# Attention by column norms and a top-1 mixture of experts on one core: hand-outs one row group sooner, raw weights in pieces, norms in columns

## The chip, the cores and the metric

The kernel runs on one core of a Trainium2 chip. Its time is device microseconds (us) of one execution. Three runs of the kernel before took 1202.16, 1208.28 and 1210.1 us; the median is 1208.28. The profiled execution is a separate one.

## The reference

For each of 4 batches, q, k and v are 5056 x 256. Norms run over the 5056 rows (`axis=1`), so the attention matrix is 256 x 256:

```python
qn = q / (np.linalg.norm(q, axis=1, keepdims=True) + 1e-06)
kn = k / (np.linalg.norm(k, axis=1, keepdims=True) + 1e-06)
s = kn.transpose(0, 2, 1) @ qn / tau
a = np.exp(s - s.max(-1, keepdims=True))
a /= a.sum(-1, keepdims=True) + 1e-09
x = (v @ a).reshape(20224, 256)
e_idx = np.argmax(x @ w_gate, axis=1)          # 8 experts
# out[i] = prob(e) * sigmoid(x_i @ w_output_gate)[e] * (relu(x_i @ w1[e]) @ w2[e]), w1 256x1024, w2 1024x256
```

## The kernel before, in words

**Gram.** `gram(b)` loads q and k in 20 steps of two 128-row tiles (tag `qk`, 6 buffers), squares and adds them for the norms (L353, L354), and multiplies k by q in fp32 (L366): the Gram product. After the last step it sums the squares over the partitions (L381 for q as a row of 256, L383 for k as two columns), takes the root on ScalarE (L389), refines and inverts it in seven VectorE instructions on 258 columns (L390 to L397), scales, and makes the softmax, its transpose and the product with the gate matrices. Pauses (`HOLD`) stand between these, so that other work comes in between.

**Mixing.** `mix(b)` makes v @ a in 20 steps of 256 rows: four transposes of v (L477), twelve matmuls (L506 to L508), the copies L481, L483 and L509. A row group is four steps (1024 rows; the fifth and last group has 960). After each group `route` finds each row's expert, counts ranks within the expert with small matmuls (L576, L579), and eight indirect DMAs of GpSimd scatter the rows, 256 values and gates, to the expert's region in DRAM (L598).

**Hand-out.** `checkpoint(n)` reads the counts so far. It orders the experts by size (`rank_experts`), writes a mark behind the scatters (L615), and makes a table of the next blocks of 256 tokens (`table`, `weights`): checkpoint 0 after `mix(1)` gives 4 blocks, checkpoint 1 after `mix(2)` gives 10, checkpoint 2 the rest. Before the last one, only blocks that are full for certain may be given out; `FIRST[r]` is the first block that may use the expert of rank r: 0, 4, 11, 18, 25, 32, 39, 46.

**Weights.** `prep` loads an expert's two matrices (1 MB each, L273, L276), and `split` squares and sums them for a scale (L297), then makes a high and a low fp16 half (L310 on ScalarE, L311 on VectorE) and stores both to DRAM (L316). Rank 0 is split in place into the weight buffer; the others go by one buffer `sp` and one `sl`. The raw matrices of ranks 0 and 1 use the tag `raw` (3 buffers, shared with the hidden activations `hb` of a block); the later ones use `st`, the buffers of mixed rows.

**Blocks.** `blocks` runs one block in four turns of PE work: h = relu(x w1) in three fp16 products (L919 to L921), y = h w2 likewise (L942 to L944). Rows are fetched on SP's queue (L843, into `qk` buffers), transposed by DMA on SP's queue (L885), weights are fetched on GpSimd's queue where the expert changes (L825), results scattered (L954).

**Order.** The program's order is written by hand with Python generators: the loops at L1012 to L1055 step `mix`, and beside each step draw so many steps of the Gram work (`ahead`, `GRATE` 1.3), of `prep` and of `run` (the blocks). The framework's planner then orders each engine's instructions by its own cost estimates, within the dependences. Each engine, and each engine's queue of DMA issues, then works through its instructions in that order. Counting `yield`s: a `mix` has 23, a `gram` 32; before, Gram work lasts until about step 10 of `mix(2)`; `run` is drawn from step `OPEN` = 10 on, and its first nine draws (`FAR` 5, then 1 + `XP` + `NEAR`) hold no matmuls.

```python
    some = checkpoint(0)
    next(some)                                  # ranks, counts, mark: after mix(1)
    preps = prep(0, AHEAD)
    for b in range(SOON, B - 1):                # b = 2
        for i, _ in enumerate(_steps(mix(b), (ahead, GRATE), (preps, PRATE))):
            if i == LATE: finish(some); opened[0] += 1     # table
            if i >= OPEN: next(run)
```

Of the kernel before, what the change touches and what calls it, by code (L numbers as in the profile page):

```python
# [20 lines left out]
P = 128  # L21
BLK = 256
BIG = 4194304
EXP_MASK = 0x7F800000

# [19 lines left out]
def tile_colnorm_attention_then_top1_moe(  # L45
# [45 lines left out]
    sure = [-(-(n * N - E * (BLK - 1)) // BLK) for n in (SOON, B - 1)]  # L91
# [165 lines left out]
    def prep(first, end):  # L257
# [3 lines left out]
        def gather():  # L261
            r, half = jobs[len(raws)]
            if r > AHEAD:
                raw = wk.tile([P, R, CW], F32, tag="st", name=f"raw{r}_{half}", bufs=STB)
                raw = raw.rearrange("p r w -> p (r w)")[:, :HW1]
            else:
                raw = big.tile([P, HW1], F32, tag="raw", name=f"raw{r}_{half}", bufs=3)
            row = nc.values_load(
# [3 lines left out]
            if half == 0:  # L272
                nc.sync.dma_start(raw, wraw[0][bass.ds(row, P), :])  # L273
            else:
                rows = wraw[1][bass.ds(row, P), :].rearrange("(f a) (b d) -> (a b) f d", f=FC, d=C)
                nc.sync.dma_start(raw.rearrange("p (f d) -> p f d", f=FC), rows)  # L276
            raws.append(raw)

        for n, (r, half) in enumerate(jobs):
            while len(raws) < min(n + DEEP, len(jobs)):  # L280
                gather()
                yield
            yield from pause(LAG if n == 0 else REST)
            yield from split(raws[n], half, r)

    def split(raw, half, r):
# [8 lines left out]
        for i in range(2):  # L295
            a = slice(i * HW1 // 2, (i + 1) * HW1 // 2)
            nc.scalar.activation(hi[:, a], raw[:, a], AF.Square, accum_out=ss[:, i : i + 1])  # L297
# [9 lines left out]
        src, dh, dl = raw, hi, lo  # L307
        cuts = [(slice(None), slice(i * HW1 // 2, (i + 1) * HW1 // 2)) for i in range(2)]
        for i, a in enumerate(cuts):
            nc.scalar.activation(dh[a], src[a], AF.Copy, scale=sw)  # L310
            nc.vector.scalar_tensor_tensor(  # L311
                out=dl[a], in0=src[a], scalar=sw, in1=dh[a], op0=ALU.mult, op1=ALU.subtract
            )
# [11 lines left out]
    def gram(b):  # L325
# [55 lines left out]
        nc.tensor.matmul(k_ps[:, :C], onesf, both[:, 0, :], start=True, stop=True, skip_group_check=True)  # L381
        for c in range(CC):
            nc.tensor.matmul(  # L383
                k_ps[:, C + c : C + c + 1], both[:, 1, c * P : (c + 1) * P], onesf[:, 0:1],
                start=False, stop=c == CC - 1, skip_group_check=True,
            )
        ss = k_ps[:, : C + CC]
        root = one.tile([P, C + CC], F32, tag="root", name=f"root{b}")
        nc.scalar.activation(root, ss, AF.Sqrt)  # L389
        nc.vector.tensor_scalar(out=root, in0=root, scalar1=1e-30, scalar2=None, op0=ALU.max)  # L390
        r = one.tile([P, C + CC], F32, tag="rq", name=f"rn{b}")
        nc.vector.reciprocal(r, root)
        nc.vector.tensor_tensor(out=r, in0=ss, in1=r, op=ALU.mult)
        nc.vector.tensor_tensor(out=r, in0=r, in1=root, op=ALU.add)
        nc.vector.tensor_scalar(out=r, in0=r, scalar1=0.5, scalar2=1e-6, op0=ALU.mult, op1=ALU.add)
        nc.vector.tensor_scalar(out=r[:, C:], in0=r[:, C:], scalar1=tau_b, scalar2=None, op0=ALU.mult)
        nc.vector.reciprocal(r, r)  # L397
# [694 lines left out]
```

## Time and profile before

| what | value |
|---|---|
| median of three runs | 1208.28 us |
| profiled execution | 1209.88 us, of which the span 1208.1 us |
| TensorE (PE) busy | 1174.4 us (97%) |
| VectorE (DVE) / ScalarE (ACT) / GpSimd (POOL) busy | 748.5 / 602.3 / 517.9 us |
| mean granted TensorE clock | 0.990 of 2.4 GHz |
| DMA | 208.56 MB |

The span is from the first instruction to the last. A busy PE here is PE with matmuls under way; the table by stage below shows where it stood idle, and at which clock.

### The profile page before, as it was taken

The numbers are of one execution on the slowest core, as the hardware profiler recorded it, in microseconds if no ns is written. First come the engines' busy times: TensorE is split into PE (matmuls) and PEld (weight loads), VectorE is DVE, ScalarE is ACT, GpSimd is POOL, SyncE is SP. The second block draws the span as 40 slices with busy tenths as digits, with TensorE's granted clock in tenths as the row PEclk, the third lists the DMA queues.
The fourth block names the chain that finished last, engine by engine and source line by source line (L and its number), as shares of the span: only waits on it lengthen the run. The fifth ranks groups of instructions, "written<-read, shape, count | busy, mean of one in ns | idle before, by whom it ended". The sixth has DMA issues, their size and how long they took to land.

```text
span 1208.1 us, 28097 instructions
## 1 busy us (share of the span) xinstructions
PE 1174.4 (97%) x10412; PEld 1066.4 (88%) x10412; DVE 748.5 (62%) x2300; ACT 602.3 (50%) x1193; POOL 517.9 (43%) x518
## 2 busy tenths in 40 slices
PE   8999999997997999999999999999999999999997
PEld 7899999887996888888888888888889999999997
DVE  7787768788685966566666654555554555555531
ACT  6576656576574555555556443333333444344432
POOL 0003756536565753333444433344444444444433
PEclk9999999998998999999999999999999999999999
DMA  9976888877767898657554436643325534336533
GB/s 319 330 246 207 301 277 259 295 242 215 212 242 236 223 264 178 150 147 174 148 137 126 112 80 113 182 76 77 72 63 176 112 73 82 79 81 197 168 104 130
DMA packets 186307, 208.56 MB, mean 173 GB/s; under 512 B 121832, under 2 KB 134510, under 8 KB 182200
## 3 DMA queue, kind: packets, MB, share of 16 engines
q1 hardware_dynamic: 145368, 139.41, 42.0%
q0 software_dynamic: 40512, 67.05, 18.9%
q8 instruction: 84, 1.38, 0.5%
q14 instruction: 55, 0.45, 0.1%
q10 hardware_dynamic: 288, 0.26, 0.1%
HBM read 281.84 MB, written 61.41 MB: 284 GB/s over the span
## 4 chain that ended last, share of the span: by engine, by line
PE 87%; DMA 6%; DVE 2%; issue 2%; ACT 1%; SPq 1%; POOL 0%; POOLq 0%; DVEq 0%; ACTq 0%
PE h_ps L919 11%; PE h_ps L921 11%; PE h_ps L920 11%; PE y_ps L942 11%; PE y_ps L943 11%; PE y_ps L944 11%; PE s_ps L366 10%; PE x_ps L506 3%; PE x_ps L508 2%; PE x_ps L507 2%; PE vt_ps L477 2%; DMA wbuf<-wsc,wi 1%; DMA qk<-in_k_dram 1%; DMA raw<-in_moe_w_dram 1%; DMA qk<-in_q_dram 1%
## 5 line engine op out<-in xcount | busy, mean ns | idle before, releaser
L924 DVE SCALAR_TENSOR_TENSOR hb<-h_ps,hb 128x512 f16<-128x512 f32 (+1 forms) x360 | 228.5, 636 | 276.0 <-ACT hb L923 275.1
L923 ACT ACTIVATE hb<-h_ps 128x512 f16<-128x512 f32 (+1 forms) x360 | 197.9, 552 | 364.1 <-PE h_ps L921 362.5
L919 PE MATMUL h_ps<-xt,wbuf 128*128 128x256 f16 (+1 forms) x1440 | 366.5, 262 | 3.0 <-ACT st L509 3.0
L921 PE MATMUL h_ps<-xt,wbuf 128*128 128x256 f16 (+1 forms) x1440 | 366.6, 262 | 0.0
L920 PE MATMUL h_ps<-xt,wbuf 128*128 128x256 f16 (+1 forms) x1440 | 366.5, 262 | 0.0
L942 PE MATMUL y_ps<-wbuf,hb 128*128 128x256 f16 x1296 | 353.3, 273 | 5.0 <-ACT yo L948 2.4
L944 PE MATMUL y_ps<-wbuf,hb 128*128 128x256 f16 x1296 | 353.3, 273 | 0.0
L943 PE MATMUL y_ps<-wbuf,hb 128*128 128x256 f16 x1296 | 353.3, 273 | 0.0
L825 POOL DMA_INDIRECT wbuf<-wsc,wi x172 | 177.8, 1034 | 404.5 <-PE h_ps L921 365.2
L598 POOL DMA_INDIRECT xs_d<-st,r_si x160 | 168.1, 1051 | 199.2 <-DVE r_d L550 101.9
L954 POOL DMA_INDIRECT out_dram<-yo,b_id x162 | 165.4, 1021 | 69.2 <-issue 42.3
L366 PE MATMUL s_ps<-qk 128*128 128x256 f32 x640 | 152.4, 390 | 5.8 <-DMA qk<-in_q_dram 3.9
L920 PEld LDWEIGHTS <-wbuf 128*128 128x128 f16 x1440 | 141.0, 98 | 16.9 <-issue 3.2
L919 PEld LDWEIGHTS <-wbuf 128*128 128x128 f16 x1440 | 142.1, 99 | 14.1
L921 PEld LDWEIGHTS <-wbuf 128*128 128x128 f16 x1440 | 141.1, 98 | 13.3
L943 PEld LDWEIGHTS <-hb 128*128 128x128 f16 x1296 | 126.8, 98 | 19.3 <-issue 5.6
L366 PEld LDWEIGHTS s_ps<-qk 128*128 128x128 f32 x640 | 121.4, 196 | 21.2 <-DMA qk<-in_k_dram 3.9
L944 PEld LDWEIGHTS <-hb 128*128 128x128 f16 x1296 | 126.8, 98 | 14.9
L942 PEld LDWEIGHTS <-hb 128*128 128x128 f16 x1296 | 126.8, 98 | 14.3
L354 DVE TENSOR_TENSOR acc<-acc,sq 128x1024 f32<-128x1024 f32 x76 | 92.9, 1223 | 46.8 <-ACT sq L353 45.4
L880 ACT ACTIVATE xr<-xg,b_sx 128x256 f16<-128x256 f32 x162 | 74.6, 502 | 66.8 <-DVE b_sx L233 46.4
L353 ACT ACTIVATE sq<-qk 128x1024 f32<-128x1024 f32 x76 | 80.3, 1060 | 53.0 <-DMA qk<-in_k_dram 44.8
(191 smaller groups left out, 1448.8 us busy)
## 6 DMA issues: line engine op xcount, KB each, us to landing
xg<-xs_d SPq DMA_DIRECT2D x72, 272.0 KB
qk<-in_q_dram SPq DMA_DIRECT2D x75, 256.0 KB
qk<-in_k_dram SPq DMA_DIRECT2D x75, 256.0 KB
v<-in_v_dram SPq DMA_DIRECT2D x32, 512.0 KB
raw<-in_moe_w_dram SPq DMA_DIRECT2D x16, 1024.0 KB
wsc<-whi SPq DMA_DIRECT2D x14, 512.0 KB
wsc<-wlo SPq DMA_DIRECT2D x14, 512.0 KB
v<-in_v_dram SPq DMA_DIRECT2D x8, 480.0 KB
```

The costliest lines, as they stand in the source:

```text
L366: nc.tensor.matmul(s_ps[:, c, :], kt[:, 1, t, c * P : (c + 1) * P], qt[:, 0, t, :], start=st == 0 and t0 == 0 and t == 0 and c == 0 and n ...
L598: ins = nc.gpsimd.indirect_dma_start(out=xs_d[:, :], out_offset=bass.IndirectOffsetOnAxis(ap=si[:np_, t : t + 1], axis=0), in_=st[:np_, t, ...
L825: nc.gpsimd.indirect_dma_start(out=wbuf[half][:, at_of(u), :], out_offset=None, in_=wsc[half][:end, :], in_offset=bass.IndirectOffsetOnAxi ...
L919: nc.tensor.matmul(hp, w1s[:, 0, c, fs], xh, start=fi == 0 and c == 0, stop=False, **KWM)
L920: nc.tensor.matmul(hp, w1s[:, 0, c, fs], xl, start=False, stop=False, **KWM)
L921: nc.tensor.matmul(hp, w1s[:, 1, c, fs], xh, start=False, stop=fin, **KWM)
L923: nc.scalar.activation(hh, h_ps[:, :, :w], AF.Relu)
L924: nc.vector.scalar_tensor_tensor(out=hb[:, 1, 2 * fp : 2 * fp + 2, :w], in0=h_ps[:, :, :w], scalar=0.0, in1=hh, op0=ALU.max, op1=ALU.subtract,
L942: nc.tensor.matmul(y_ps[:, t, :], hb[:, 0, f, tsl], w2s[:, 0, f, :], start=st, stop=False, **KWM)
L943: nc.tensor.matmul(y_ps[:, t, :], hb[:, 0, f, tsl], w2s[:, 1, f, :], start=False, stop=False, **KWM)
L944: nc.tensor.matmul(y_ps[:, t, :], hb[:, 1, f, tsl], w2s[:, 0, f, :], start=False, stop=fin, **KWM)
L954: ins = nc.gpsimd.indirect_dma_start(out=out[:, :], out_offset=bass.IndirectOffsetOnAxis(ap=un["id"][:, t : t + 1], axis=0), in_=un["yo"][ ...
```

## The change

1. **Hand-outs.** Checkpoints 0 and 1 are split over hooks in `mix(1)` and `mix(2)`: ranks and counts are read in step 18, before the last row group is counted; the mark is written at the end of the same `mix`, ahead of the last group's scatters; the table follows in step `LATE` = 1 (was 5) of the next. The last group's 960 rows are left out of the sure blocks, so `FIRST` becomes 0, 4, 11, 17, 23, 30, 36, 42. `OPEN` goes from 10 to 3.
2. **Raw weights.** Each raw matrix is loaded as two pieces of 512 KB, each half stored as soon as it is split; ranks from 2 on use the `v` buffers (4 of 512 KB) instead of `st`. `prep` of rank 0 starts in step 18 of `mix(1)`, of rank 1 in step 18 of `mix(2)`; then comes a pause of 22 draws.
3. **Norms.** Four column sums of one column each; an integer estimate and two Newton steps for the reciprocal root, plus one correction of the root, on 4 columns on VectorE in place of the ScalarE root; a diagonal matrix and an fp32 matmul bring q's factors back to a row.
4. **Rates.** 1.4 Gram steps to a step of `mix(0)` and `mix(1)` (was 1.3); other rates as below; rows are fetched at every turn of a block, not once per block.

```diff
-    sure = [-(-(n * N - E * (BLK - 1)) // BLK) for n in (SOON, B - 1)]
+    sure = [-(-(n * N - (N - (NG - 1) * GROUP) - E * (BLK - 1)) // BLK) for n in (SOON, B - 1)]
-    GRATE = 1.3
+    GRATE, AHEAD_RATE = 1.3, 1.4
-    DEEP, LAG, REST = 2, 3, 2
-    LATE, OPEN, MARKED = 5, 10, 3
+    DEEP, LAG, REST, SLOW = 2, 4, 1, 4
+    LATE, OPEN, MARKED, HOOKED = 1, 3, 3, 18
+    REST_AT = 22
-    BRATE = 0.7
+    BRATE = 0.72
-    MRATE = 1.2
-    WRATE = 0.8
+    MRATE = 1.8
+    WRATE = 1.0
...
             if r > AHEAD:
-                raw = wk.tile([P, R, CW], F32, tag="st", name=f"raw{r}_{half}", bufs=STB)
+                parts = [
+                    ld.tile([P, 4, C], F32, tag="v", name=f"raw{r}_{half}_{i}", bufs=VB).rearrange("p t c -> p (t c)")
+                    for i in range(2)
+                ]
...
+            for i, part in enumerate(parts):
+                if half == 0:
+                    nc.sync.dma_start(part, rows[:, i * HW1 // 2 : (i + 1) * HW1 // 2])
...
+                yield
...
-            yield from pause(LAG if n == 0 else REST)
+            yield from pause(LAG if n == 0 else SLOW if r > AHEAD + 1 else REST)
...
+            for n, part in enumerate((hi, lo)):
+                nc.sync.dma_start(wsc[half][rows, n * HW1 + a.start : n * HW1 + a.stop], part[:, a])
             yield
-        for n, part in enumerate((hi, lo)):
-            nc.sync.dma_start(wsc[half][rows, n * HW1 : (n + 1) * HW1], part)
...
-        nc.tensor.matmul(k_ps[:, :C], onesf, both[:, 0, :], start=True, stop=True, skip_group_check=True)
+        for i in range(2):
+            for c in range(CC):
+                n = i * CC + c
+                nc.tensor.matmul(
+                    k_ps[:, n : n + 1], both[:, i, c * P : (c + 1) * P], onesf[:, 0:1],
...
+        nc.vector.tensor_scalar(
+            out=y.bitcast(I32), in0=half, scalar1=-1.0, scalar2=float(RSQRT), op0=ALU.mult, op1=ALU.add
+        )
+        for _ in range(2):
+            t = t4("n_t")
+            nc.vector.tensor_tensor(out=t, in0=hss, in1=y, op=ALU.mult)
+            nc.vector.tensor_tensor(out=t, in0=t, in1=y, op=ALU.mult)
+            nc.vector.scalar_tensor_tensor(out=y, in0=t, scalar=1.5, in1=y, op0=ALU.add, op1=ALU.mult)
...
-        nc.scalar.activation(root, ss, AF.Sqrt)
...
-        nc.vector.reciprocal(r, root)
...
+        nc.vector.reciprocal(r, r)
+        dq = one.tile([P, CC, P], F32, tag="root", name=f"dq{b}")
         for c in range(CC):
+            nc.vector.tensor_scalar(out=dq[:, c, :], in0=ident, scalar1=r[:, c : c + 1], scalar2=None, op0=ALU.mult)
+        yield from pause(HOLD + 1)
+        n_ps = ps_x.tile([P, 512], F32, tag="x", name=f"n_ps{b}")
+        nc.tensor.matmul(n_ps[:, :C], onesf, dq.rearrange("p c m -> p (c m)"), start=True, stop=True)
+        yield
+        rq, rk = n_ps[:, :C], r[:, CC:]
...
+                adv("x", fetch_x, got["prep"] + QKB)
...
     for b in range(SOON, B - 1):
-        for i, _ in enumerate(_steps(mix(b), (ahead, GRATE), (preps, PRATE))):
+        for i, _ in enumerate(_steps(mix(b, hand[1]), (ahead, GRATE))):
+            if i < HOOKED:
+                due += PRATE
+                while due >= 1.0:
+                    due -= 1.0
+                    next(preps, None)
+            else:
+                if i == HOOKED:
+                    finish(preps)
+                    preps = chain(prep(AHEAD, AHEAD + 1), pause(REST_AT), prep(AHEAD + 1, E))
+                next(preps)
             if i == LATE:
-                finish(some)
+                finish(hand[0])
                 opened[0] += 1
             if i >= OPEN:
-                next(run)
+                some += 1.0 if i < OPEN + FAR + XP + 1 + NEAR else BRATE
+                while some >= 1.0:
+                    some -= 1.0
+                    next(run)
```

## Rows read from the trace of the kernel before

**Rows 1.** The page's first part: busy us, share of the span and instructions of each engine.

```profile
PE 1174.4 (97%) x10412; PEld 1066.4 (88%) x10412; DVE 748.5 (62%) x2300; ACT 602.3 (50%) x1193; POOL 517.9 (43%) x518
```

**Rows 2.** Busy time by stage. Columns: stage in us from the span's start, its length, busy us (and instructions) of PE, its weight loads, DVE, ACT, POOL, then the granted share of TensorE's clock, the DMA engines' busy share, and GB/s.

```profile
0.00:75.00 75.00, 69.16 (x321) 60.53 (x322) 55.45 (x80) 48.69 (x55) 2.72 (x19) 0.98 0.93 316
75.00:220.00 145.00, 144.52 (x1035) 135.72 (x1034) 107.66 (x289) 95.12 (x203) 74.45 (x69) 1.00 0.80 256
220.00:250.00 30.00, 25.91 (x176) 23.86 (x175) 18.39 (x78) 17.85 (x36) 12.09 (x13) 0.94 0.84 292
...
272.00:300.00 28.00, 20.84 (x169) 19.53 (x168) 22.28 (x87) 17.28 (x41) 16.53 (x18) 0.88 0.80 220
...
360.00:385.00 25.00, 17.44 (x131) 15.35 (x131) 14.13 (x62) 12.04 (x27) 12.73 (x13) 0.86 0.86 268
385.00:430.00 45.00, 43.36 (x404) 38.85 (x403) 37.55 (x153) 22.46 (x42) 34.76 (x33) 1.00 0.81 210
430.00:1184.00 754.00, 753.75 (x7311) 680.41 (x7310) 423.87 (x1287) 331.00 (x660) 312.20 (x305) 1.00 0.51 126
1184.00:1208.10 24.10, 17.67 (x184) 15.72 (x182) 4.47 (x8) 5.71 (x12) 7.33 (x8) 0.95 0.35 123
```

**Rows 3.** The same view for two short stretches in which the clock was low.

```profile
286.00:293.00 7.00, 3.94 (x25) 3.95 (x26) 5.56 (x29) 2.75 (x10) 5.48 (x6) 0.60 0.76 194
380.00:383.00 3.00, 3.00 (x15) 2.33 (x14) 0.59 (x2) 1.05 (x4) 0.38 (x2) 0.51 0.64 202
```

**Rows 4.** The chain of waits, 205 to 320 us: start, length, what.

```profile
229.96 0.14 DVE ri L771
...
231.09 8.47 DMA raw<-in_moe_w_dram
```

**Rows 5.** ACT in order of time around 231 us; in brackets the idle time before an instruction and what ended it.

```profile
239.59 1.06 ACT L297 ACTIVATE wbuf<-raw 128x1024 f16<-128x1024 f32 x1 [7.00 <-DMA raw<-in_moe_w_dram]
```

**Rows 6.** The same chain, 271 to 290 us of it.

```profile
271.59 0.43 PE k_ps L381 x2
272.02 0.34 PE k_ps L383 x4
...
276.14 1.68 DVE rn L392
...
284.86 1.67 DVE rn L397
...
288.87 0.14 DVE r_oh L556
```

**Rows 7.** ACT in order of time, 272 to 276 us.

```profile
272.74 1.28 ACT L389 ACT_TABLE_LOAD   x1
274.03 0.39 ACT L389 ACTIVATE root<-k_ps 128x258 f32<-128x258 f32 x1
274.43 1.28 ACT L567 ACT_TABLE_LOAD   x1
```

**Rows 8.** First and last start (us) of the Gram matmuls and of the first matmul of a block: duration ns min/median/max, first and last start.

```profile
L366 PE MATMUL s_ps<-qk x640: 377/379/774, 3.9 to 264.9; 128*128 128x256 f32 x160
L919 PE MATMUL h_ps<-xt,wbuf x1440: 219/272/418, 296.0 to 1198.1; 128*128 128x256 f16 x144, 128*128 128x128 f16 x36
```

**Rows 9.** The same chain, 248 to 251 us of it: what one step of mixing and two thirds of a Gram step take of PE.

```profile
248.41 0.44 PE vt_ps L477 x4
248.84 0.13 PE x_ps L506
...
250.35 1.73 PE s_ps L366 x8
```

**Rows 10.** ACT in order of time, 364 to 378 us.

```profile
371.62 0.51 ACT L880 ACTIVATE xr<-xg,b_sx 128x256 f16<-128x256 f32 x1 [7.06 <-DMA xt<-xr]
...
377.33 1.06 ACT L297 ACTIVATE whi<-raw 128x1024 f16<-128x1024 f32 x1 [1.19 <-DMA wsc<-whi]
```

**Rows 11.** SP's queue in order of time, 358 to 371 us.

```profile
358.11 0.39 SPq L276 DMA_DIRECT2D raw<-in_moe_w_dram  x1
...
360.39 9.85 SPq L885 DMA_TRANSPOSE xt<-xr  x4
370.34 0.53 SPq L316 DMA_DIRECT2D wsc<-whi  x1
```

**Rows 12.** The chain of waits at two fetches of weights.

```profile
417.37 5.52 DMA wbuf<-wsc,wi
...
754.93 11.69 DMA wbuf<-wsc,wi
```

**Rows 13.** Groups of instructions by line: count | busy us, mean ns of one | idle before.

```profile
L392 DVE RECIPROCAL rn<-root 128x258 f32<-128x258 f32 x4 | 7.0, 1762 | 0.1
L390 DVE TENSOR_SCALAR root<-root 128x258 f32<-128x258 f32 x4 | 1.4, 348 | 3.5 <-ACT root L389 3.5
L562 DVE TENSOR_SCALAR r_se<-r_se 128x8 f32<-128x8 f32 x20 | 4.1, 203 | 0.1
L598 POOL DMA_INDIRECT xs_d<-st,r_si x160 | 168.1, 1051 | 199.2 <-DVE r_d L550 101.9 <-issue 40.8 <-ACT st L509 18.0
```

**Rows 14.** What SP's queue waited for: us in total, times, longest.

```profile
SPq L276 <- DMA xs_d<-st,r_si: 18.5, 2, 9.4
SPq L268 <- DVE tb_ni L666: 6.0, 1, 6.0
```

More of the change, by code (lines that the diff above doesn't have):

```diff
@@ L24 @@
 EXP_MASK = 0x7F800000
+RSQRT = 0x5F3759DF
 def _beside(main, *others):
@@ L271, in gather @@
             )
[L272 to L277, printed above, removed]
+            rows = wraw[half][bass.ds(row, P), :]
+            for i, part in enumerate(parts):
+                if half == 0:
+                    nc.sync.dma_start(part, rows[:, i * HW1 // 2 : (i + 1) * HW1 // 2])
+                else:
+                    nf = FC // 2
+                    of = rows.rearrange("(f a) (b d) -> (a b) f d", f=FC, d=C)[:, i * nf : (i + 1) * nf, :]
+                    nc.sync.dma_start(part.rearrange("p (f d) -> p f d", f=nf), of)
+                yield
         for n, (r, half) in enumerate(jobs):
             while len(raws) < min(n + DEEP, len(jobs)):
-                gather()
-                yield
-            yield from pause(LAG if n == 0 else REST)
+                yield from gather()
+            yield from pause(LAG if n == 0 else SLOW if r > AHEAD + 1 else REST)
             yield from split(raws[n], half, r)
@@ L380, in gram @@
         k_ps = ps_x.tile([P, 512], F32, tag="x", name=f"k_ps{b}")
-        nc.tensor.matmul(k_ps[:, :C], onesf, both[:, 0, :], start=True, stop=True, skip_group_check=True)
-        for c in range(CC):
[L383 to L388, printed above, removed]
@@ L397, in gram, with t4 @@
-        nc.vector.reciprocal(r, r)
-        yield from pause(HOLD)
-        rq, rk = r[:, :C], r[:, C:]
+        for i in range(2):
+            for c in range(CC):
+                n = i * CC + c
+                nc.tensor.matmul(
+                    k_ps[:, n : n + 1], both[:, i, c * P : (c + 1) * P], onesf[:, 0:1],
+                    start=n == 0, stop=n == 2 * CC - 1, skip_group_check=True,
+                )
+        def t4(tag, dt=F32):
+            return sm.tile([P, 2 * CC], dt, tag=tag, name=f"{tag}{b}")
@@ L453, in tile_colnorm_attention_then_top1_moe, with mix @@
     left = [None]
-    def mix(b):
+    def mix(b, hook=None):
         later = None
@@ L514, in mix @@
                 sow(1)
+                if g == NG - 1 and hook:
+                    next(hook)
             yield
@@ L521, in mix @@
         sow(R)
+        if hook:
+            next(hook)
         finish(later)
@@ L779, in checkpoint @@
         of_rank(rcr, rc)
+        if not last:
+            yield
         open_marks(ck)
@@ L1042, in tile_colnorm_attention_then_top1_moe @@
             next(run)
-    finish(preps)
-    some = checkpoint(1)
-    next(some)
-    preps = prep(AHEAD, E)
     for i, _ in enumerate(_steps(mix(B - 1), (run, BRATE), (preps, MRATE))):
         if i == LATE:
-            finish(some)
+            finish(hand[1])
         if i == LATE + MARKED:
```

47 lines of the change are left out of this document (29 added, 18 removed).

## The prediction

> **What bounds the kernel now.** I read the engines' busy shares first: PE is busy for 1174.4 of 1208.1 us, the next engine for 62% [rows 1]. So the time is PE's own work plus what PE stands idle, 33.7 us, plus what it loses at the lower clock. The change takes nothing from PE's work; it can only win idle time and clock. The busy time by stage says where these lie [rows 2]: from 430 to 1184 us PE idles 0.25 us in all, from 75 to 220 us 0.48. The start (5.8 us up to 75 us) and the tail (6.4 us from 1184 us) are not touched. What is left, three stretches and a rest: 4.1 us in 220 to 250, 7.2 in 272 to 300, 7.6 in 360 to 385, 1.6 in 385 to 430, together 20.5 us. All lie where mixing, hand-out, weights and first blocks overlap. In the first three the granted share is 0.94, 0.88 and 0.86: after each idle stretch the clock stood at 1.2 GHz for some microseconds. All of that lost share would be 1.8 + 3.4 + 3.5 = 8.7 us, but part of it fell on idle time. In 286 to 293 PE was busy 3.94 of 7 us at 0.60, in 380 to 383 all the time at 0.51 [rows 3], which is about 1.6 and 1.5 us of lost work; I take 5.5 us for the three, between 3.1 and 8.7. The pool to be won is 20.5 + 5.5 = 26 us, at most 29.
>
> The waits name the causes. **A** (220 to 250): the order of experts is ready on VectorE at 229.96 us, the first raw load goes out at 231.09 and takes 8.47 us [rows 4]; ScalarE, with the squares of that load next in its order, stands 7.00 us [rows 5], and with it the copies that mixing needs. **B** (272 to 300): the Gram matmuls end at 264.9 us and the first block's matmuls start at 296.0 [rows 8], so PE has mixing alone to do, and mixing hangs on VectorE. There two reciprocals of 1.7 us and the rest of the norms stand in a row ahead of the one-hot that PE's rank matmuls need at 288.87 us [rows 6]; ScalarE spends 2.6 us on two table loads for one root [rows 7]. **C** (360 to 385): on SP's queue four transposes take 9.85 us beside a raw load of 1 MB issued 2 us before, and a weight store waits behind them [rows 11]; ScalarE stands 7.06 us for a transpose and 1.19 us for the store [rows 10]. **D**: a fetch of weights at 417.37 us takes 5.52 us, with PE behind it [rows 12].
>
> **The change, part by part.** *Hand-out earlier (A, D).* The ranks move from after `mix(1)` to its step 18, some 5 steps. A step holds 0.44 + 12 x 0.125 = 1.94 us of mixing on PE and 1.4 Gram steps of 1.73 us [rows 9], 4.36 us, so 22 us. The first square follows the first raw load by eight draws: five steps of `mix(1)` and 2.5 of `mix(2)`, over 30 us, where load and wait took 8.5. I count A's 4.1 + 1.3 us as won but for 0.5. What moves along: about fourteen VectorE instructions of 0.2 us for the ranks, 2.8 us, and some 25 for the table, 5 us [rows 13]; in the earlier place there is Gram work on PE to cover them. The loads' row number is read on SP, which stood 6.0 us for it [rows 14]; the q, k and v loads stand behind. Six `qk` buffers last 6/1.4 steps, 18.7 us, so that is hidden; without that cover it would cost its 6 us. The mark now stands ahead of the last group's eight scatters on GpSimd, with at most the landing of the scatters before it; nobody needs those scatters before the four `st` buffers run out. The early row fetches take four of the six `qk` buffers from step 3 of `mix(2)`, while about six Gram steps are still to load. With two buffers a Gram step comes every (5.5 + 1.1 + 1.7)/2 = 4.1 us, with a load like the 5.52 us fetch [rows 12], a square and the products [rows 5, 9]; with (1.94 + 1.3 x 1.73)/1.3 = 3.2 wanted, six steps lose between 0 and 5 us. I take 1, since the fetches can be planned behind the loads.
>
> *Filler for mixing (B).* `run` starts at step 3 instead of 10, and after nine draws its matmuls come at step 12 instead of 19. Of the Gram work, 14 + 32 + 32 draws are made before `mix(2)` (12 + 29 + 30 before), and 10 of the last batch's 20 loading steps are left instead of 13: at 1.3 a step they end at step 8 instead of 10. So the steps without filler fall from nine to four or five. In such a step GpSimd's two scatters, 2 x 1.05 us [rows 13], exceed PE's 1.94, so they cannot be free: of 7.2 + 1.7 us I keep 45%, 4 us.
>
> *Norms.* On VectorE the two reciprocals, 3.5 us, and five more, about 1.8, give way to some 18 instructions on 4 columns at 0.14 to 0.2 us [rows 4, 13] and two of 128 columns at 0.2 to 0.35: 2.9 to 4.3, so from 5.3 to about 3.7 us a batch. ScalarE loses a root and two table loads. On PE four columns at 0.17 us and one fp32 product of 0.43 take the place of 0.43 + 0.34 [rows 6]: 1.11 for 0.77, four times, **+1.4 us** on PE, with no cover. The chain's gain is hidden for three batches under Gram work; for the fourth it lies in B: 1.6 us of VectorE and up to 2.6 of ScalarE, of which I take 1 us. So B gives 8.9 - 4 + 1, about 6 us.
>
> For the table loads the row decides: 1.28 us each, the next instruction 0.01 us later [rows 7]. The Trainium skill (ScalarE: Activation LUTs, "What ACT_TABLE_LOAD costs") adds a drain of about 1.38 us to each switch, 2.66 in all; the trace does not show that drain, and by the page B would give some 2.7 us more.
>
> *Weights (C, D).* Rank 1's loads come in steps 18 to 21 of `mix(2)`, its splits in the first eight steps of `mix(3)`; the pause of 22 draws puts the next raw load at step 20 of `mix(3)`, so the 1 MB beside the transposes is gone, and each store needs only its half. But stores and transposes still share SP's queue, and a split now issues six DMAs, not three, at 0.39 to 0.53 us each [rows 11], in front of the transposes that ScalarE waits for. I keep a third of C's 7.6 + 2.5 us, and win 6.7. D's 1.6 is won: by the draws rank 1's first half is split at step 5 of `mix(3)` and block 4 wants it at step 11, six steps of at least 3.7 us later (1.94, and 0.72 of a quarter block). Later ranks: rank 2 is ready when block 9.75 runs, block 11 fetches it. A block's 96 matmuls at 754/7311 us [rows 2] are 10 us, so that leaves 12, against a store of some 6 and a fetch of 5.52 to 11.69 [rows 12], with h needing only the first half and y a block later; margins grow by half a block per rank.
>
> **The sum.** 4.9 + 6 + 6.7 + 1.6 = 19.2 won, less 1.4 and 1.0 lost: 16.8 us off 1209.88, 1193.1. The profiled execution was 1.6 us above the median of the runs, so **1191 us**.
>
> **Rivals.** *The stalls only move* (0.20): the planner orders by its own estimates, and has been wrong on exactly these waits; a load planned as landed can again stop ScalarE, now at step 18 of `mix(1)` or in `mix(3)`. For it: A was such a case. Against: PE has Gram work there. Half of the 19.2 us stays, plus the lost 2.4: about 1201 us.
>
> *Pieces cost more than they hide* (0.07): 16 loads and 32 stores more. For ranks 0 and 1 that is 12 more DMAs where PE is not dense; each costs SP 0.4 us [rows 11], and if each delayed a transpose by as much as a fixed cost near the 1.19 us wait of the store [rows 10], 5 to 14 us go back: about 1202 us. It is what the Trainium skill (DMA: Bandwidth & Descriptors, "Rules for kernel authors") would say, at least 1 MiB per DMA, with about 2 us fixed for each; in the trace the 1 MB load reached only 1 MB in 8.47 us among other traffic [rows 4], so size was not what limited it there.
>
> *Slower: the ring of `raw`* (0.11). At the end of `mix(2)` it has to hold two blocks' `hb` and both of rank 1's raw matrices, four tiles in three buffers. Block 2's `hb` waits for a split that stands four steps into `mix(3)`. If the planner puts that block's matmuls ahead of it, PE's four accumulator banks fill and mixing stops too. Price: the load of 8.47 us and five passes over half a matrix at 1.06 [rows 4, 5], 13.8 us, for blocks 2 and 3, and 1.7 us of clock after each: 31 us, 1191 + 31 = 1222. It decides from about 29 us on. For it: SP's second raw load already waits 9.4 us [rows 14]. Against: before has the same two loads beside blocks 0 and 1, and PE hardly idled there.
>
> *Forecast* (0.62): 1180 to 1196.
>
> **Chances and range.** A difference below about 1%, 12 us, can't be told from no change here: the runs spread by 8 us. Faster by more, below 1196.2: the forecast, 0.62. Within 1%: the first two rivals, 0.27. Slower, above 1220.4: the third, 0.11. Low end: all of the 29 us won, less 1.4, is 1180.7; 3 us for the runs' spread makes 1177. High end: 1213, which takes in both middle rivals with that spread and half of the ring's price; some 0.1 lies above it, less below 1177.
>
> **What would show it.** Right: no wait over 2 us of ScalarE for a raw load; PE idle between 220 and 430 us below 9 us with at most one stretch at the lower clock; the first block's matmuls no more than 20 us behind the last Gram matmul; no table load for a root; 430 onwards as dense as before. Wrong: PE waiting for copies right after a Gram end or for `hb`, Gram matmuls waiting for q and k loads in the first steps of `mix(2)`, or PE waiting for weights at blocks 11, 17 or 23.

## The result and the profile after

The changed kernel takes **1216.55 us** (median of 12 runs, 1210.97 to 1221.67), the kernel before 1207.83 (12 runs, 1202.16 to 1211.48). The ratio is **1.0077, interval 1.0056 to 1.0098**: by my bound within 1%, but clear of no change, and on the other side of it than the 1191 us that I forecast. The profiled execution took 1217.97 us, 8.1 more than that of before.

The page's first lines; [rows 1] are those of before:

```profile
span 1216.3 us, 28279 instructions
...
PE 1178.5 (97%) x10428; PEld 1067.3 (88%) x10428; DVE 732.7 (60%) x2348; ACT 594.0 (49%) x1181; POOL 516.9 (42%) x518
```

VectorE and ScalarE did lose work (748.5 to 732.7, 602.3 to 594.0), in the direction that I had counted. PE has 4.1 us more of busy time and 4.1 more of idle time. To place them, the busy time of both kernels in the same four stages. The figure in brackets behind PE's busy time is the number of PE's matmul records; from 445 to 1190 us one comes every 0.103 us (744.10 us busy, 7221 records), so it measures how far the work has come. A record that lies across an edge counts in both stages. After:

```profile
0.00:200.00 200.00, 193.66 (x1229) 177.81 (x1229) 143.09 (x362) 126.30 (x224) 63.23 (x75) 1.00 0.82 276
200.00:300.00 100.00, 90.98 (x655) 84.14 (x655) 72.42 (x290) 59.09 (x128) 52.67 (x50) 0.97 0.79 250
300.00:395.00 95.00, 85.95 (x736) 77.75 (x735) 62.20 (x264) 53.10 (x124) 51.17 (x52) 0.96 0.74 227
395.00:445.00 50.00, 46.16 (x413) 40.34 (x411) 33.63 (x136) 20.69 (x40) 35.40 (x35) 0.97 0.64 182
```

Before:

```profile
0.00:200.00 200.00, 193.68 (x1219) 177.75 (x1220) 147.71 (x322) 131.13 (x229) 65.16 (x76) 0.99 0.85 278
200.00:300.00 100.00, 88.75 (x634) 82.61 (x633) 77.03 (x287) 62.86 (x140) 51.85 (x54) 0.95 0.81 254
300.00:395.00 95.00, 87.22 (x771) 80.13 (x770) 65.27 (x274) 55.67 (x126) 53.83 (x53) 0.96 0.73 227
395.00:445.00 50.00, 48.36 (x445) 43.24 (x444) 39.93 (x154) 25.92 (x46) 33.98 (x32) 1.00 0.91 254
```

Taken as one stretch, 0 to 395 us has 2616 records in either kernel, and 16 of the changed kernel's are extra ones of the norms: it is 16 records, 1.6 us, behind. From 395 to 445, where mixing is over in both but for its last 2 us in the changed kernel, it falls another 32 records, 3.3 us, behind. That is 5 of the 8.2 us of span. The other 3 lie behind 445 us: PE idles 9.6 us there, before 6.7. In e12 below, nearly the same program, it is 7.4, so how much of this belongs to the change is open.

Taken together, the three stretches that were to give 17.6 us gave about 1 us of idle time (19.0 us from 200 to 395 us before, 18.1 after), and the fourth, D, which was to give 1.6 us, became a loss of 2.2 us idle. But the first three did not stand still. PE's idle time in finer stretches (length less PE's busy time):

| stretch, us | before | after |
|---|---|---|
| 220 to 250 (A) | 4.1 | 3.2 |
| 250 to 272 | 0.0 | 2.7 |
| 272 to 300 (B) | 7.2 | 3.1 |
| 300 to 345 | 0.2 | 7.4 |
| 360 to 385 (C) | 7.6 | 1.4 |
| 385 to 430 (D) | 1.6 | 4.1 |

The stalls of B and C fell by 4.1 and 6.1 us, and new ones came where there had been none. The rows of the largest, before and then after, and of C after ([rows 2] has C before):

```profile
300.00:345.00 45.00, 44.78 (x408) 41.62 (x407) 31.76 (x138) 26.43 (x60) 23.18 (x23) 1.00 0.83 258
```

```profile
300.00:345.00 45.00, 37.63 (x307) 34.20 (x306) 29.00 (x133) 24.99 (x58) 20.91 (x22) 0.93 0.77 247
360.00:385.00 25.00, 23.57 (x210) 21.15 (x209) 12.22 (x45) 12.52 (x31) 14.42 (x15) 1.00 0.74 198
```

**A, again.** The ranks are ready at 214 us in place of 230, the first raw load goes out at 215.0, and ScalarE, in order of time, again has the squares next and stands for it (in brackets the idle time and what ended it; [rows 5] is before):

```profile
220.31 1.06 ACT L305 ACTIVATE wbuf<-raw 128x1024 f16<-128x1024 f32 x1 [4.75 <-DMA raw<-in_moe_w_dram]
...
221.82 1.06 ACT L305 ACTIVATE wbuf<-raw 128x1024 f16<-128x1024 f32 x1 [0.36 <-DMA raw<-in_moe_w_dram]
...
224.00 1.06 ACT L305 ACTIVATE wbuf<-raw 128x1024 f16<-128x1024 f32 x1 [1.03 <-DMA raw<-in_moe_w_dram]
```

That is 6.1 us in sum, where before had 7.6, the same stall 19 us earlier (the first square starts at 220.31 us; 239.59 in [rows 5]).

**B, with other waits.** SP's queue in order of time and then the chain of waits: four row fetches (`xg`) stand 4.99 us on SP ahead of the last q, k and v loads, and then a v load and a k load are on the chain that ended last; PE waits 0.8 us for the k load and 1.9 us for the sum of squares behind it.

```profile
231.84 4.99 SPq L878 DMA_DIRECT2D xg<-xs_d  x4
```

```profile
250.42 7.02 DMA v<-in_v_dram
257.84 4.24 DMA qk<-in_k_dram
262.19 1.06 ACT sq L360
263.28 1.23 DVE acc L361
```

The last Gram matmul starts at 264.1 us (264.9 before) and the first block's at 281.4 (296.0): the blocks do come earlier, by 14.6 us.

**C and D, on POOL's queue.** POOL in order of time, first in 308 to 333 us:

```profile
308.71 0.97 POOL L631 DMA_INDIRECT xs_d<-st,r_si  x1 [0.30 <-issue]
317.03 0.58 POOL L648 DMA_DIRECT2D mark<-xs_d  x1 [7.35 <-issue]
319.89 1.02 POOL L631 DMA_INDIRECT xs_d<-st,r_si  x1 [2.28 <-DMA mark<-xs_d]
...
329.30 0.99 POOL L631 DMA_INDIRECT xs_d<-st,r_si  x1 [0.30 <-issue]
330.60 1.01 POOL L989 DMA_INDIRECT out_dram<-yo,b_id  x1 [0.30 <-ACT xr L915]
```

The mark stands 7.35 us, the scatter behind it another 2.28, then come the last row group's eight scatters, 1.3 us each, and only then the first block's output. That output (`yo`) was ready at 316.3 us, so it stood 14.3 us in the queue. Its buffers are those of the transposed v: ScalarE's next `vh` waits 3.38 us for the output, behind it stands the copy to `st`, and PE waits 3.9 us for that copy. (The chain of waits there goes through a weight store that landed at 339.84 us; e12 takes up that reading.) ScalarE in order of time, and PE's waits in 75 to 480 us (total, times, longest):

```profile
315.48 0.85 ACT L983 ACTIVATE yo<-y_ps,b_gs 128x256 f32<-128x256 f32 x2
...
338.27 0.59 ACT L510 CAST vh<-vt_ps 128x512 fp32r<-128x512 f32 x1 [3.38 <-DMA out_dram<-yo,b_id]
```

```profile
PE x_ps L535 <- ACT st L538: 8.9, 8, 3.9
PE h_ps L954 <- DMA wbuf<-wsc,wi: 3.8, 2, 3.4
```

Before, the mark waits as well, but behind the group's scatters and with nothing in a hurry behind it; the output then found POOL idle:

```profile
314.14 0.99 POOL L598 DMA_INDIRECT xs_d<-st,r_si  x1 [0.31 <-issue]
319.63 0.59 POOL L615 DMA_DIRECT2D mark<-xs_d  x1 [4.50 <-DMA xs_d<-st,r_si]
325.21 0.99 POOL L954 DMA_INDIRECT out_dram<-yo,b_id  x1 [4.99 <-ACT yo L948]
```

The last line of PE's waits is D. POOL in 406 to 420 us:

```profile
406.59 1.05 POOL L860 DMA_INDIRECT wbuf<-wsc,wi  x1 [0.30 <-PE y_ps L979]
407.94 1.03 POOL L631 DMA_INDIRECT xs_d<-st,r_si  x1 [0.31 <-DVE tb_at L669]
...
417.12 1.00 POOL L631 DMA_INDIRECT xs_d<-st,r_si  x1 [0.30 <-ACT hb L958]
418.43 1.11 POOL L860 DMA_INDIRECT wbuf<-wsc,wi  x1 [0.30 <-issue]
```

POOL goes from one DMA to the next without a pause, and the fetch at 418.43 that PE wants for the weights of the next block stands behind eight scatters that began at 407.94. The weight buffer that it fills was free: the last matmuls that read it ended at 406.3 us.

### The profile page after: what moved, and what is told of

It reads as the page before. It is cut to its first block, busy times and chain, and to the rows that moved or that the text cites. A ratio compares the mean times of both kernels' runs of the same rounds, so it can differ in the third digit from the quotient of the medians.

```text
span 1216.3 us, 28279 instructions
## 1 busy us (share of the span) xinstructions
PE 1178.5 (97%) x10428; PEld 1067.3 (88%) x10428; DVE 732.7 (60%) x2348; ACT 594.0 (49%) x1181; POOL 516.9 (42%) x518
## 4 chain that ended last, share of the span: by engine, by line
PE 82%; DMA 8%; issue 4%; ACT 2%; DVE 2%; POOL 1%; SPq 0%; POOLq 0%; ACTq 0%; DVEq 0%
PE h_ps L954 11%; PE h_ps L956 11%; PE h_ps L955 11%; PE y_ps L977 10%; PE y_ps L979 10%; PE y_ps L978 10%; PE s_ps L373 8%; PE x_ps L535 2%; DMA qk<-in_k_dram 2%; PE x_ps L537 2%; PE x_ps L536 2%; PE vt_ps L506 2%; DMA xs_d<-st,r_si 1%; DMA wbuf<-wsc,wi 1%; DMA out_dram<-yo,b_id 1%
## 5 line engine op out<-in xcount | busy, mean ns | idle before, releaser
L373 PE MATMUL s_ps<-qk 128*128 128x256 f32 x640 | 148.7, 384 | 5.8 <-DMA qk<-in_q_dram 3.9
L955 PEld LDWEIGHTS <-wbuf 128*128 128x128 f16 x1440 | 141.2, 98 | 14.3 <-issue 0.3
L535 PE MATMUL x_ps<-ah,vh 128*128 128x272 f32 x320 | 102.9, 324 | 13.5 <-ACT st L538 8.9
```

The lines of the kernel that those rows point to most:

```text
L373: nc.tensor.matmul(s_ps[:, c, :], kt[:, 1, t, c * P : (c + 1) * P], qt[:, 0, t, :], start=st == 0 and t0 == 0 and t == 0 and c == 0 and n ...
L955: nc.tensor.matmul(hp, w1s[:, 0, c, fs], xl, start=False, stop=False, **KWM)
```

## The experiments

The 18 runs were made in five groups, each on one chip beside runs of the kernel before. In two groups before takes 1207.7 us, as in its profile (e9 to e12; e17, e18); in three 1262 to 1270 (e1 to e4; e5 to e8; e13 to e16). The expectations speak of a "slower chip"; what makes the difference is not known, one chip number turned up with either time. Each ratio is to the runs of before in the same group, and medians are compared only at the same level of before.

**The parts alone, before at 1270 us.**

e1_norms, only the norms:

```diff
-        nc.scalar.activation(root, ss, AF.Sqrt)
...
+            nc.vector.scalar_tensor_tensor(out=y, in0=t, scalar=1.5, in1=y, op0=ALU.add, op1=ALU.mult)
```

> The kernel before with the norms of the change alone (column sums, root on VectorE, one fp32 product to bring q's factors back). Theory 'moved waits' (the loss comes from where hand-out, raw loads and row fetches now stand): between 1204 and 1210 us, since 1.4 us of PE come on top and the chain of the last batch gets 1 to 4 us shorter. Rival 'norms' (the extra products and one more accumulator bank in use cost the 9 us): 1214 to 1218 us.

1.0015 (0.9991 to 1.0039): no difference.

e2_rate, only 1.4 Gram steps in the first two batches:

```diff
-        _beside(mix(b) if b else first, (ahead, GRATE))
+        _beside(mix(b) if b else first, (ahead, 1.4))
```

> The kernel before with 1.4 Gram steps to a mixing step in the first two batches alone. 'Moved waits': 1205 to 1211 us, the three stretches with stalls as before. Rival 'rate' (Gram work that ends earlier leaves longer stretches without filler, PE idles more in 265 to 300 us): 1212 to 1218 us.

1.0088 (1.0056 to 1.0120), slower by itself.

e3_pieces, only loads and stores in halves:

```diff
-                nc.sync.dma_start(raw, wraw[0][bass.ds(row, P), :])
+                    nc.sync.dma_start(part, rows[:, i * HW1 // 2 : (i + 1) * HW1 // 2])
...
+                nc.sync.dma_start(wsc[half][rows, n * HW1 + a.start : n * HW1 + a.stop], part[:, a])
```

> The kernel before with raw weights loaded in two pieces each and every half stored as soon as it is split, buffers and times as before. 'Moved waits': 1203 to 1209 us; ScalarE's wait for the first raw load falls from 7.0 to about 5 us. Rival 'pieces' (twice the DMAs on SP's queue hold up transposes and loads): 1212 to 1218 us.

1.0010 (0.9973 to 1.0046): no difference.

e4_handout, the changed kernel without norms, pieces and the rate (the raw matrices of later ranks are in `st` again; of the diff, the rate and one line of the loads):

```diff
-    GRATE, AHEAD_RATE = 1.3, 1.4
+    GRATE, AHEAD_RATE = 1.3, 1.3
...
-                yield from gather()
+                gather()
```

> The changed kernel with the norms, the whole raw loads and stores and the Gram rate of the kernel before: what is left is the earlier hand-out, the earlier weights of ranks 0 and 1 and the earlier blocks and row fetches. 'Moved waits': 1214 to 1220 us, with ScalarE standing over 5 us for the first raw load at about 215 us. Each of the three rivals: at most 1210 us here.

1.0097 (1.0063 to 1.0131). At this level the moved hand-out with its earlier blocks is a loss of the size of the whole.

e15_rest, the complement, in a later group (before at 1262 us): before with norms, pieces and the rate 1.4 together (the diffs of e1, e2 and e3).

> The kernel before with everything of the change but the hand-out and the blocks' times: norms in columns, loads and stores in pieces in the buffers of before, and 1.4 Gram steps. Theory "hand-out and blocks" (they alone are the loss): 0.998 to 1.002. Rival "rate" (1.0088 alone on the slower chip of the first call): 1.004 to 1.010.

1.0017 (0.9987 to 1.0047). Together the three cost nothing that can be measured here, so with e4 it is the hand-out and the blocks that make the loss at this level (e11 below puts a question to this at the other one). That the rate alone gave 1.0088 does not add up with this, and stays open.

**Which part of the hand-out, before at 1269 us.**

e5_after, the changed kernel itself, no diff.

> The changed kernel itself, as the base that the three runs beside it are read against on the same chip. All theories: 1.005 to 1.012 of the kernel before. If this chip shows the spread issue waits of the first four experiments (before at 1270 us), the ratio may lie at the upper end.

1.0115 (1.0063 to 1.0168).

e6_rate135:

```diff
-    GRATE, AHEAD_RATE = 1.3, 1.4
+    GRATE, AHEAD_RATE = 1.3, 1.35
```

> The changed kernel with 1.35 Gram steps drawn to a mixing step of the first two batches, halfway back from 1.4 to 1.3. Theory "rate" (the denser Gram steps are the loss; alone they gave 1.0088): half of it comes back, 0.996 of the changed kernel or lower, 1.003 of the kernel before. Theory "moved waits" (the hand-out, the weights and the row fetches stand at the wrong place whatever the rate): 0.998 to 1.002 of the changed kernel.

1.0145 (1.0088 to 1.0202). The median is 1.8 us above e5_after: a sign against the rate, but with five runs of each, spread over 13 to 15 us, 0.996 is not shut out.

e7_pin:

```diff
-            nc.scalar.activation(hi[:, a], raw[i], AF.Square, accum_out=ss[:, i : i + 1])
+            with tc.issue_after(left[0].ins) if left[0] is not None else nullcontext():
+                nc.scalar.activation(hi[:, a], raw[i], AF.Square, accum_out=ss[:, i : i + 1])
```

> The changed kernel, each half of a block's squares issued only behind the mixing copy that is the latest at its place in the program, so that the planner can't put it right behind its own estimate of the load. Theory "squares too soon": ACT's 6 us of waits for the raw load at 220 us fall below 1 us, TensorE's 3.4 us gap at 222 us goes with its lower clock, and the time is 3 to 6 us below the changed kernel (0.995 to 0.9975 of it). Rival "stalls only move": the wait for the load goes, but the first weights are split later and TensorE stands for them or for the copies behind them before 300 us: 0.999 to 1.004 of the changed kernel.

1.0109 (1.0062 to 1.0157), e5_after 1.0115. Between 210 and 260 us no wait of ScalarE for the raw load is left; whether the 3 to 6 us came back these intervals are too wide to tell. And in e5_after's trace the idle time in front of that square is put to "issue", not to the load, so I tried the same where the load's wait shows (e9).

e8_open10:

```diff
-    LATE, OPEN, MARKED, HOOKED = 1, 3, 3, 18
+    LATE, OPEN, MARKED, HOOKED = 1, 10, 3, 18
```

> The changed kernel with the blocks drawn from step 10 of the last mixing stages but one on, as before, not from step 3, so that the first four row fetches stand on SP behind the q and k loads. Theory "fetch first" (row fetches that wait 5 us on SP ahead of the q, k and v loads make the waits at 250 to 268 us): the 4.2 and 7.0 us steps for qk and v leave the chain, TensorE's idle time in 250 to 300 us falls from 5.8 to under 3 us, and the time is 2 to 4 us below the changed kernel (0.9965 to 0.9985). Rival "first block late": the first block starts some 15 us later, as before the change, and its filler is missing in the Gram's end: 1.000 to 1.005 of the changed kernel.

1.0070 (1.0040 to 1.0101): the median is 7.9 us below e5_after, but the intervals overlap. In its trace PE idles 2.8 us in 250 to 300 us (e5_after 4.8), as "fetch first" expected; the chain can't tell, since neither trace has a q, k or v load on it there. A hint that the early blocks cost, no more.

**Before at 1207.7 us, as in the profiles.**

e9_pinbefore, the kernel before with the edit of e7.

> The kernel before with each half of a block's squares issued only behind the latest mixing copy, nothing else changed. Theory "stall of its own" (the step of my prediction that took the 7.0 us wait of ACT for the raw load at 231 us for lost time that comes back when the load is there in time): the wait falls below 1 us and the time is 3 to 5 us below the kernel before (0.996 to 0.9975). Rival "stalls only move" (the squares in the changed kernel, pinned, gave 0.998 of it, within the noise): 0.999 to 1.004, with the wait found again at TensorE's next wait for a copy.

0.9999 (0.9980 to 1.0018). ScalarE in order of time: the squares now start with their load landed, no idle time in front of them.

```profile
236.59 1.06 ACT L298 ACTIVATE wbuf<-raw 128x1024 f16<-128x1024 f32 x1
...
237.65 1.04 ACT L298 ACTIVATE wbuf<-raw 128x1024 f16<-128x1024 f32 x1
```

So stall A, 7.6 us of ScalarE and 4.1 us of PE in the trace, is worth at most 2.4 us by itself (the interval's end), and the 3 to 5 us expected are shut out. By its number that is the rival "stalls only move"; where the time went instead, the trace does not show. The profiled run is a trap here: it took 1202.01 us, the shortest of 11 whose median is 1207.11, and read alone would have shown a gain of 8 us.

e10_handopen, e4_handout with the blocks from step 10 (the diff of e8).

> The kernel of the fourth run (hand-out, weights and blocks moved, without the norms, the pieces and the rate 1.4; 1.0097 of the kernel before) with the blocks drawn from step 10 on again. Theory "early blocks" (it is the row fetches and blocks from step 3 on that cost, not the hand-out): half or more of the 1.0097 comes back, 1.000 to 1.005 of the kernel before. Rival "hand-out itself" (the rank search and the raw loads ahead of the last row group): 1.007 to 1.012.

1.0019 (1.0000 to 1.0038), which is what "early blocks" expected; but e4_handout ran at the other level, so this does not show by itself that the early blocks are the loss. The stage behind mixing tells more, the same as above, and PE's only wait in it:

```profile
395.00:445.00 50.00, 45.40 (x403) 39.96 (x401) 37.76 (x136) 24.08 (x43) 31.14 (x31) 0.97 0.73 204
```

```profile
PE h_ps L928 <- DVE tb_ok L735: 4.6, 1, 4.6
```

Up to 395 us this kernel has 2639 records, 23 more than before: here 2.4 us are won. From 395 to 445 it has 42 fewer, 4.3 us. (h does not read `tb_ok`; POOL issued the fetch of its weights at 405.18, behind eight scatters from 394.12 on, and PE went on at 407.4.)

e11_openpin, the changed kernel with the edits of e7 and e8.

> The changed kernel with both edits of the last call: blocks from step 10 on (alone 1.007 of the kernel before) and pinned squares (alone 1.0109). If the two losses are separate: 1.003 to 1.006 of the kernel before. If the pinned squares only move the stall: 1.006 to 1.009.

1.0060 (1.0033 to 1.0088): no lower than the changed kernel by more than the noise; PE waits 6.5 us for `wbuf` in 395 to 445 us. Beside e10 it is 4.1 us slower, though the intervals still touch. The two differ by the norms, the pieces with their buffers, the rate 1.4 and the pinned squares, the first three of which e15 had found to cost nothing at the other level. In e11's trace PE waits 3.8 us for the norms' diagonal matrix (`dq`); the changed kernel's trace has 0.8 us of wait at that place. So at this level these parts may cost some of the loss.

e12_junk:

```diff
-            nc.scalar.activation(hi[:, a], raw[i], AF.Square, accum_out=ss[:, i : i + 1])
+            out = hi[:, a] if r == 0 else one.tile([P, CC, C], F32, tag="at", name="junk").rearrange("p c m -> p (c m)").bitcast(F16)
+            nc.scalar.activation(out, raw[i], AF.Square, accum_out=ss[:, i : i + 1])
```

> The changed kernel with the squares of the second and later blocks written into another buffer (that of the transposed scores, idle there), so that they needn't wait until the stores of the row block before have read the high halves. Theory "one buffer": ACT's 6.7 us wait for the store at 333 us goes and with it TensorE's 4.0 us gap at 336 us, 0.996 to 0.998 of the changed kernel, 1.004 to 1.009 of the kernel before here. Rival "stalls only move": the copy that follows waits for the same store; 1.009 to 1.014 of the kernel before.

1.0087 (1.0058 to 1.0115), in both ranges, and 1217.23 us is not below the changed kernel's 1216.55. In its trace ScalarE waits for no store there, and the gap at 336 us is gone but for 0.7 us (at 339.7); but PE has gaps of 2.6 us at 326.6 and 2.7 us at 358.9, and the time is no lower. The chain at 333 us now goes through the output scatter (4.60 us). From ScalarE's row above I read the changed kernel's gap as the wait for the output; this run does not settle whether the store had a part in it, only that its going gave no time.

**POOL's queue.** At this level all four traces with the hand-out moved (after, e10, e11, e12) have 32 to 56 records less than before in 395 to 445 us, with a wait for weights of 3.8 to 6.5 us; e9 has 3 less. Test: the last row group's scatters are drawn between the blocks' draws, so that fetches get ahead of them.

e13_spread, in the changed kernel, and e14_spreadbefore, the same edit in the kernel before:

```diff
-        sow(R)
+        for _ in range(R):
+            sow(1)
+            if b == B - 1:
+                yield
```

> The changed kernel with the eight scatters of the last row group drawn one at a time between the draws of the blocks, so that two pairs of weights fetches stand ahead of them on POOL. Theory "POOL's queue" (TensorE's wait for wbuf at 418 us is a fetch that POOL reaches only behind eight scatters of 1.3 us): the second of the two waits, 2.5 to 5 us in the traces with the hand-out moved, goes, units 5 to 9 take 42 to 45 us in place of 48, and the time is 3 to 5 us below the changed kernel, 1.003 to 1.006 of the kernel before. Rival "weights late at their source" (the fetch would wait for the stores of the scaled weights anyway): 1.007 to 1.010.

> The kernel before with the same edit. Theory "POOL's queue": its wait for wbuf at 421 us is 1.8 us, so at most 2 us come back, 0.998 to 1.000. Rival: the scatters that come later delay the table of the remaining blocks and TensorE stands for it, 1.002 to 1.006.

e16_spreadopen, the same edit in e10_handopen:

> The hand-out alone with the blocks from step 10 on (1.0019 of the kernel before) and the spread scatters. Theory "POOL's queue": its 4.8 us gap at 402 us goes, 0.997 to 1.000 of the kernel before, the first version below it. Rival "weights late at their source": 1.001 to 1.004.

Before took 1262 us here: 1.0089 (1.0057 to 1.0121), 1.0033 (1.0004 to 1.0062) and 1.0056 (1.0029 to 1.0084). The first two lie in their rivals' ranges, the third above both. At that level e5_after, without the spread, shows no wait for `wbuf` between 75 and 480 us either, so these can't decide on the queue; in the kernel before the edit may cost a little. The last two runs repeat e13 and e16, with before at 1207.8 us.

> The changed kernel with the spread scatters again, for a chip on which the wait for wbuf behind the scatters shows (the kernel before at about 1208 us). Theory "POOL's queue": no wait for wbuf over 1 us at 400 to 425 us, units 5 to 9 in 42 to 45 us (48.0 in the changed kernel), 1.003 to 1.006 of the kernel before. Rival "weights late at their source" or "the loss moves on": 1.007 to 1.010. If the kernel before takes 1260 us here, 1.007 to 1.011 by both, and nothing is settled.

**e17_spread2: 1.0044 (1.0024 to 1.0065)**, 1212.84 us, 3.7 below the changed kernel. POOL in order of time, PE's waits in 395 to 445 us, the stage:

```profile
405.23 0.97 POOL L635 DMA_INDIRECT xs_d<-st,r_si  x1 [0.30 <-issue]
406.50 1.05 POOL L864 DMA_INDIRECT wbuf<-wsc,wi  x1 [0.30 <-issue]
407.86 1.01 POOL L864 DMA_INDIRECT wbuf<-wsc,wi  x1 [0.31 <-issue]
...
423.12 1.03 POOL L635 DMA_INDIRECT xs_d<-st,r_si  x1 [0.30 <-DVE hb L963]
```

```profile
PE h_ps L958 <- DMA wbuf<-wsc,wi: 1.9, 1, 1.9
```

```profile
395.00:445.00 50.00, 48.07 (x447) 42.93 (x447) 37.58 (x160) 26.22 (x49) 36.47 (x34) 1.00 0.76 204
```

Up to 395 us the trace is that of the changed kernel (2618 records to 2616); then it makes 447 records, two more than before. Blocks 5 to 9 (the expectations' units) take 44.5 us in place of 48.0, as the theory expected. The 34 records are 3.5 us, and the medians differ by 3.7, with intervals that overlap.

> The hand-out alone, blocks from step 10 on, with the spread scatters, for the same chip. Theory "POOL's queue": the 4.8 us gap at 402 us goes, units 5 to 9 in 42 to 45 us (47.2 without the spread), 0.996 to 1.000 of the kernel before. Rival: 1.001 to 1.004. If the kernel before takes 1260 us here, 1.003 to 1.008 as in the last call.

**e18_spreadopen2: 1.0082 (1.0052 to 1.0112)**, where without the spread it was 1.0019. It is worse than either theory expected, and its trace shows the same queue; then the chain's row of the last fetch, PE's wait and the stage:

```profile
411.64 1.02 POOL L609 DMA_INDIRECT xs_d<-st,r_si  x1 [0.32 <-DVE tb_n L675]
...
423.05 1.01 POOL L609 DMA_INDIRECT xs_d<-st,r_si  x1 [0.30 <-issue]
424.36 1.27 POOL L655 DMA_INDIRECT xs_d<-void,tb_ei  x1 [0.30 <-issue]
425.94 0.98 POOL L655 DMA_INDIRECT xs_d<-void,tb_ei  x1 [0.30 <-issue]
427.23 1.05 POOL L838 DMA_INDIRECT wbuf<-wsc,wi  x1 [0.30 <-PE h_ps L934]
```

```profile
427.23 9.83 DMA wbuf<-wsc,wi
```

```profile
PE h_ps L932 <- DMA wbuf<-wsc,wi: 8.7, 1, 8.7
```

```profile
395.00:445.00 50.00, 38.50 (x346) 33.19 (x343) 36.01 (x149) 22.18 (x41) 32.73 (x27) 0.93 0.68 194
```

The gap at 402 us is gone, but two blocks later a fetch stands behind the eight scatters and the two of the void rows (its line names PE, but the matmuls that last read its buffer, those of the block two before, had ended by 417.3 us), and PE stands 8.7 us. The queue is not all of that: the fetch goes out 1.2 us before PE runs out of work, and then takes 9.83 us, where the changed kernel's two took 2.45 and 2.51. Why is not known. In the stage it has 57 records less than e10, 5.9 us; the medians differ by 8.3. So the same edit gave about 3.7 us back in one kernel and cost 8.3 in another, and in both traces PE's wait in this stretch follows from which fetch stands behind the scatters. No run beat the kernel before by more than the noise.

## Why the prediction was wrong

**The pool** (20.5 us of idle time and 5.5 of clock) was the right place: the stalls that went and those that came lie in 200 to 445 us, but for 2.9 us of idle time behind it. But I took its stalls for time that comes back when their cause goes: that is the step that failed. PE's idle time in 200 to 445 is 21.9 us after and 20.7 before, where the sum had 19.2 us won (clock included). I summed what each moved step frees; for what it then stands in front of I put 1.0 us on SP and nothing on POOL.

**A, 4.9 us won: failed, and twice.** "The first square follows the first raw load by eight draws ... over 30 us": draws are places in the program, not times. The planner orders each engine by its own estimates, and put the squares right behind its estimate of the load; 6.1 of 7.6 us of waiting stayed. And the premise, that PE's 4.1 us would be won, fell with e9: with the wait gone the time is 0.9999 (0.9980 at the least).

**B, 6 us won, 1.0 lost to row fetches: half right.** The first block starts 17 us behind the last Gram matmul, as I had put it as a sign, and the two VectorE reciprocals and the ScalarE root left the chain. In 272 to 300 us PE idles 4.1 us less. But "I take 1, since the fetches can be planned behind the loads" was too little: they stood ahead of the last ones, and 250 to 272 us, dense before, has 2.7 us of idle time. That the fetches make it is argued from SP's order and the chain; e8, at the other level, only hints at it. In all, PE's idle time in 200 to 300 us fell by 2.2 us where A and B, less the 1.0, were to give 9.9, part of it in clock.

**Norms, +1.4 us on PE:** their groups have 6.5 us of busy time for 4.5, +2.0, and e1 differs by 1.9 us, within its noise. This term was about right, 0.6 us too small; of the 1 us that I let them win in B, e1 shows nothing. Of nine table loads of 1283 ns one is left, and e1 shows no gain: the drain that the Trainium skill adds to each (ScalarE: Activation LUTs, "What ACT_TABLE_LOAD costs") would have made a gain larger, and no run here shows one.

**C, 6.7 us won: failed.** The stall itself went, from 7.6 to 1.4 us in 360 to 385, but 300 to 345 us, where PE had idled 0.2 us, has 7.4: in 300 to 395 in all the idle time rose from 7.8 to 9.1. The step that failed is the sentence on the mark: "nobody needs those scatters before the four `st` buffers run out". True of the scatters, but I asked only who waits for them, not what is queued behind them on POOL: the outputs of the early blocks, whose buffers the next copies of v need. That this is the 3.9 us gap at 336 us is read from the trace; no run took the mark away, and e12, in whose trace that gap is 0.7 us, is no faster.

**D, 1.6 us won: failed, the largest net loss.** "Six steps of at least 3.7 us later" compared the blocks with the weights' split and store. The weights were there; the fetch stood behind scatters, and PE's idle time in 385 to 430 us rose from 1.6 to 4.1. My warning sign, "PE waiting for weights at blocks 11, 17 or 23", named the wrong blocks. The earlier blocks and the mixing that ends at 397 us in place of 387 bring the last scatters and the first fetches of weights together. e17 puts about 3.7 of the 8.7 us here; e18 shows the order of the queue at work with the other sign.

**The rivals.** "The stalls only move" was nearest (1201 us): its mechanism, squares planned too early, is what A shows, but it has nothing of POOL's queue, from which I read C's and D's new stalls, and it let half of the win stand, when none did. The ring of `raw` did not show: no wait of PE for `hb` beyond 1 us. Pieces cost nothing that e3 could measure (1.0046 at the most), although they halve the loads to 512 KB. That is against the rule of at least 1 MiB per DMA in the Trainium skill (DMA: Bandwidth & Descriptors, "Rules for kernel authors"). What I lacked was a rival on the side of slower for POOL, whose 43% of busy share I took for a free engine.

**What stays open:** the rate's 1.0088 alone; how the rest of the loss, 5 us in e17, divides between norms, mark, row fetches and the 2 to 3 us more of idle time behind 445 us; whether early blocks or hand-out alone bring the scatters and the fetches together.

## What to carry to other kernels

For a step that is moved, list what is queued behind it on each engine that it uses, not only who waits for its result: an engine at 43% can stand full for 20 us just where two stages meet. A stall seen in one trace is worth what its removal gives in a run, and that may be nothing, as with A; take it away alone first. Distances counted in draws of a program that a planner reorders are no times.

## What the runs showed that I had not expected

The same program takes 5% longer in some groups of runs, in all runs of a group, and most of that lies in the mixing. PE's waits of e5_after in 75 to 480 us:

```profile
PE s_ps L373 <- issue: 8.4, 11, 2.3
PE y_ps L978 <- issue: 8.2, 8, 1.6
```

"issue" is time in which the engine waited for nothing that the profile shows; in the profile of the same kernel at 1216 us PE has no such wait in that stretch. What it is I did not find out. It can hide effects of a few microseconds in mixing: e13 and e16 told nothing of the queue, and e17 and e18 did.

On POOL an indirect DMA takes 1.0 us (median of the 496 in the changed kernel) and in a full queue the next follows after 0.30 us, whether anybody waits for it or not; the first two marks of a kernel, which read what scatters wrote, stood 4.5 to 7.9 us with the queue behind them (4.50 in the kernel before, 7.35 in the changed one, 7.91 in e17). The profile puts these waits to the scatters, the longest to "issue".
